# Moving the streamed operands of the second experts to a fixed byte offset from the weights

## The chip, the cores and the metric

The program runs on one core of one Trainium2 chip. The metric is the time of one execution in microseconds on the device. The kernel before takes 1078.79 us, the median of three runs (1077.48 to 1081.04).

## What is computed

Three stages follow each other. An attention of 2 x 8 heads over 576 positions of width 64 adds a far part (on sequences averaged by 4) and a near part (a band of 7 positions). Its result is x, 1152 tokens of width 512. A first feed-forward stage has one inner width of 2048. The second stage, the one that is touched here, has eight experts of inner width 1024, whose outputs are weighted per token by a gate that has been normalised eight times by rows and columns:

```python
# x: 1152 x 512, after attention
h = x @ w_in;  x = (h * tanh(softplus(h))) @ w_out          # first experts
P = normalised(exp(x @ w_gate))                              # 1152 x 8
out = 0
for e in range(8):                                           # second experts
    h = maximum(x @ w1[e], 0.0)
    out += P[:, e:e+1] * (h @ w2[e])
```

## The kernel before

Every fp32 matrix is held as two parts of the type that TensorE multiplies here, a high one and a low one (what the rounding left), and a product of two matrices is three matmuls: high by high, high by low, low by high. TensorE reads two operands from the on-chip memory: the weights, 128 columns that are loaded, and the streamed operand, whose columns (384 or 512 here) run past them. Each matmul has a weight load of its own.

The second experts are worked through in 22 rounds: one of a single piece of 128 inner columns, then 21 of three pieces each. In a round, the three pieces by four blocks of width by three blocks of tokens are multiplied by a scheme with 15 products of sums in place of 18 (`WSUMS`, `XSUMS` and `PROGRAM` name them). A product is six matmuls of 384 columns at line 1505. Its weights are pairs of high and low parts in eight places (`wplace`): four in the tile `wops`, one in `wop0`, two in the tile named `ysum` (`ytile` in the code), and one in `wghl`. Its streamed operand (`operand`) is a block of `xhi` and `xlo`, or a sum of blocks in `xform` or in the tile `xform8` (which the profile's rows also call `xform`, since buffer numbers are left out). ScalarE and VectorE turn the results into `hhi` and `hlo`. After that the second multiplication at line 1553 takes `hhi` and `hlo` as weights, and the streamed operand is a row of the second matrix, split into high and low parts by lines 1368 and 1370, 512 columns each. These rows rotate through three places (`cplace`): the tile `wc` (`wc0` in the code) and two in the tile `xs0`, which is called `late0` in the code and `xs` in the profile's rows. Nine token tiles with nine matmuls each make a round; VectorE adds each result to `yacc` at line 1566.

Before the first round one single piece goes through lines 1338 (its weights lie in `ysum`) and 1348 (the gate, weights in `wghl`).

The order on every engine is written out by a planner (`Plan`), which replays the steps with a table of costs and fixes the order by dependencies. Tiles get their addresses from pools in the order of their allocation. The pool `tp` lies at the upper end and grows downwards, so a tile made larger there moves those allocated ahead of it to lower addresses; in the pool `mp` it moves those allocated after it to higher ones.

In the built program these tiles start at the following bytes of each partition, given modulo 256 (`xhi` and `xlo` are at 0 in both; blocks inside a tile are 512, 1536 or 2048 bytes apart, which changes nothing modulo 256):

```
                                        before   after
weights of the products:   wops              0     192
                           ysum              0     192
                           wop0            192     192
                           wghl            192     192
streamed in the products:  xform           192       0
                           xform8            0       0
weights of line 1553:      hhi, hlo          0       0
streamed at line 1553:     wc                0      64
                           xs (late0)      192      64
```

By "offset" this document means the start of a streamed operand less the start of the weights, modulo 256 bytes. Counted over the program (it is the same count whether a streamed operand is set against its own weights or, but for the last matmul of a product or tile, against those of the next matmul):

```
offset                     0     64    192
line 1505 before         930    210    750
line 1505 after            0   1890      0
line 1553 before         597      0   1140
line 1553 after            0   1737      0
```

Of the kernel before, what the change touches and what calls it, by code (L numbers as in the profile page):

```python
# [9 lines left out]
F32R = mybir.dt.float32r  # L10
# [308 lines left out]
def attn_moe_moe_kernel(  # L319
# [15 lines left out]
    NT, DM = out.shape  # L335
# [3 lines left out]
    KD = DM // 128  # L339
    KH = KD // 2  # L340
# [26 lines left out]
    def new(pool, shape, dt, tag, bufs=2):  # L367
        return pool.tile(shape, dt, tag=tag, name=tag, bufs=bufs)
# [704 lines left out]
    tp = ctx.enter_context(tc.tile_pool(name="tp", bufs=1, side="right", reuse_waits="tile"))  # L1073
    TH = NT // 3
    xform = tp.tile([128, 8, 2, KH, TH], F32R, name="xform")
    xs = [new(tp, [128, KH, NT], F32, f"xs{k}", 1) for k in range(2)]
    wop0 = tp.tile([128, 2, KH, 128], F32R, name="wop0")
    for s in range(ATT_END, NS):
        if s == NS - 4:
            with tc.issue_after(last["mish"].ins):  # L1080
# [17 lines left out]
    mp_, m = [], {}  # L1098
# [13 lines left out]
    for r in range(2):  # L1112
        w1_load(raw1[r].t, rounds_[r])
    ytile = new(yp, [128, KD * NMAX], F32R, "ysum", 1)
    w0 = ytile[:, 0:1024].rearrange("p (z a b) -> p z a b", z=2, a=KD)
    r0 = raw1[0].t[:, 0:512].rearrange("p (a b) -> p a b", a=KD)
    ACT.activation(out=w0[:, 0], in_=r0, func=AF.Copy)
    POOL.tensor_tensor(out=w0[:, 1], in0=r0, in1=f32(w0[:, 0]), op=ALU.subtract)
# [5 lines left out]
    def wplace(i):  # L1124
        if i < 4:
            return m["wops"][:, i]
        if i == 4:
            return wop0
        if i == 7:
            return wghl.rearrange("p (z a) b -> p z a b", z=2)  # L1130
        o = 512 * (i - 5)
        return ytile[:, o:o + 512].rearrange("p (z a b) -> p z a b", z=2, a=KH)

    def cplace(i):
        return m["wc"] if i == 0 else m["late0"][:, 1024 * (i - 1):1024 * i].rearrange("p (z b) -> p z b", z=2)

    def r2place(i):
        return m["temp"][:, 512 * i:512 * i + 512]
# [1 line left out]
    def fplace(z):  # L1140
# [3 lines left out]
        return mt[:, o:o + 768] if z[0] == "m" else m["temp"][:, o:o + 768]  # L1144

    RW, RC, R2 = Ring(8, wplace), Ring(3, cplace), Ring(4, r2place)
    FR = {z: Ring(1, lambda _, z=z: fplace(z).rearrange("p (a b) -> p a b", a=KH)) for z in ("m0", "m1", "r", "t0", "t1", "t2")}
    RK = Ring(6, lambda i: m["keeps"][:, TH * i:TH * i + TH], {"k": 6})
# [146 lines left out]
    def open_():  # L1295
        gq.clear()
        ap_ctx.close()
        mp = ctx.enter_context(tc.tile_pool(name="mp", bufs=1, reuse_waits="tile"))
        mp_.append(mp)
        m["hhi"], m["hlo"] = (mp.tile([128, 3, NT], F32R, name=f"h{z}") for z in ("hi", "lo"))  # L1300
        m["yacc"] = mp.tile([128, NTL, DM], F32, name="yacc")
        m["wc"] = mp.tile([128, 2, DM], F32R, name="wc0")
        m["xform"] = mp.tile([128, 2, KH, TH], F32R, name="xform8")
        m["wops"] = mp.tile([128, 4, 2, KH, 128], F32R, name="wops")
        m["wsums"] = mp.tile([128, len(WSUMS), KH, 128], F32, name="wsums")
        m["temp"] = mp.tile([128, 2304], F32, name="temp")
        m["ones"] = mp.tile([128, 128], F32, name="ones")
        m["P"] = mp.tile([128, 80], F32, name="P")[:, 0:NTL * NE].rearrange("p (a b) -> p a b", b=NE)
    add("open", open_, w=["ap"])

    def late_():
# [43 lines left out]
    def p_rows(r, cs):  # L1355

        out_ = []
        for c in cs:
            z2, y = Buf(R2 if c else FR["t2"]), Buf(RC)
            e, f = divmod(c, NFE)  # L1360
            rk, wk = soon("r2", z2) if c else (["ap"], [])

            def raw(z2=z2, c=c):
                return z2.t if c else z2.t.rearrange("p a b -> p (a b)")[:, 0:DM]
            add("load", lambda raw=raw, e=e, f=f: SP.dma_start(out=raw(), in_=w2[e][128 * f:128 * f + 128, :]), r=rk,
                w=[("r2", c)] + wk, b=[z2], size=262144, rate=0.2)
            rk, wk = soon("c", y)
            add("whi", lambda raw=raw, y=y: ACT.activation(out=y.t[:, 0], in_=raw(), func=AF.Copy), r=[("r2", c)] + rk,  # L1368
                w=[("ch", c)] + wk, b=[z2, y])
            add("wlo", lambda raw=raw, y=y: POOL.tensor_tensor(out=y.t[:, 1], in0=raw(), in1=f32(y.t[:, 0]), op=ALU.subtract),  # L1370
                r=[("r2", c), ("ch", c)], w=[("cl", c)], b=[z2, y])
            out_.append(y)
        return out_

    wc0 = p_rows(0, [0])
# [202 lines left out]
    for r in range(1, len(rounds_)):  # L1578
# [5 lines left out]
        wc = p_rows(r, cs)  # L1584
# [34 lines left out]
```

## Time and profile before

| | before |
|---|---|
| median of three runs | 1078.79 us |
| profiled execution, its own time | 1079.52 us |
| its span, first to last instruction | 1077.7 us |
| TensorE busy | 1051.3 us, 98% of the span |
| VectorE busy | 783.2 us, 73% |
| ScalarE busy | 538.0 us, 50% |
| GpSimd busy | 445.6 us, 41% |
| mean granted clock of TensorE | 0.990 |

The profiled execution took 1.8 us more than its span, and it lies 0.7 us above the median. Matmuls are pipelined, so that a matmul's own duration is longer than the step from its start to the start of the next; how fast TensorE works is read from starts, not from durations.

### The profile page before, as it was taken

To read this page: it belongs to the slowest core of one execution; us is meant where nothing else is said; L and a number is where in the kernel's file an instruction comes from. 1 tells how busy PE (TensorE), PEld (TensorE's weight loads), DVE (VectorE), ACT (ScalarE), POOL (GpSimd) and SP (SyncE) were. 2 spreads that over 40 slices of the span, in tenths; PEclk is the share of its full clock that TensorE was granted. 3 is DMA by queue.
4 is the path that set the end of the run, shared out by engine and by line. 5 is a ranking of instruction groups with operands and counts; after the bars stand their busy time and mean duration, and the time that the engine had idled before them with its cause. 6 is when DMAs were issued, how large, how long until landed. Compare 5 with 4: busy or idle time off the path is not lost.

```text
span 1077.7 us, 18231 instructions
## 1 busy us (share of the span) xinstructions
PE 1051.3 (98%) x6770; PEld 948.5 (88%) x6770; DVE 783.2 (73%) x1394; ACT 538.0 (50%) x1429; POOL 445.6 (41%) x474
## 2 busy tenths in 40 slices
PE   8999999999988899999999999999999999999998
PEld 5799899999887798799889998889889998899887
DVE  6898865442499896887667885798677868687844
ACT  6897874343447354255434643355434544255331
POOL 0343243021158363856335643365335644355311
PEclk9999999999998899999999999999999999999999
DMA  9681222200003210111012111121111111111002
GB/s 208 178 207 47 78 79 81 96 31 30 1 11 97 60 46 33 41 58 55 25 40 60 60 24 48 47 60 36 44 40 59 59 30 50 40 59 30 20 1 88
DMA packets 48000, 63.46 MB, mean 59 GB/s; under 512 B 15272, under 2 KB 31656, under 8 KB 47912
## 3 DMA queue, kind: packets, MB, share of 16 engines
q1 hardware_dynamic: 47912, 62.30, 19.8%
q8 instruction: 53, 0.87, 0.3%
q14 instruction: 35, 0.29, 0.1%
HBM read 59.93 MB, written 2.36 MB: 58 GB/s over the span
## 4 chain that ended last, share of the span: by engine, by line
PE 83%; DVE 11%; ACT 3%; DMA 2%; issue 1%; POOL 0%; SPq 0%; DVEq 0%; ACTq 0%
PE bank L1553 35%; PE bank L1505 25%; PE bank L511 7%; PE bank L530 7%; DVE wsums L1249 3%; PE bank L946 2%; PE bank L1002 2%; DMA raw<-in_moe_w_in_dram 1%; PE bank L660 1%; ACT pl L727 1%; DVE bank L1249 1%; DVE hlo L1326 1%; DMA rawq<-in_q_dram 1%; PE bank L787 1%; PE bank L844 1%
## 5 line engine op out<-in xcount | busy, mean ns | idle before, releaser
L1566 DVE SCALAR_TENSOR_TENSOR yacc<-bank,P,yacc 128x512 f32<-128x512 f32 x208 | 152.8, 745 | 138.9 <-PE bank L1553 138.2
L1553 PE MATMUL bank<-xs,hhi 128*128 128x512 f32 (+1 forms) x760 | 239.6, 396 | 3.4 <-DVE yacc L1564 2.1
L1553 PEld LDWEIGHTS bank<-xs,hhi 128*128 128x128 f32 x760 | 142.4, 189 | 35.0 <-DVE yacc L1564 2.6
L1519 ACT ACTIVATE xs<-bank 128x384 f32<-128x384 f32 x231 | 112.7, 489 | 116.3 <-PE bank L1505 72.4
L1323 ACT ACTIVATE hhi<-bank 128x384 fp32r<-128x384 f32 x150 | 71.8, 488 | 198.0 <-PE bank L1553 193.0
L1553 PE MATMUL bank<-xs,hlo 128*128 128x512 f32 (+1 forms) x380 | 150.3, 396 | 0.0
L1553 PE MATMUL bank<-wc,hhi 128*128 128x512 f32 (+1 forms) x398 | 124.9, 395 | 0.0
L1249 DVE TENSOR_TENSOR bank<-bank,xs 128x384 f32<-128x384 f32 x189 | 101.1, 557 | 20.5 <-ACT xs L1519 16.9
L1505 PE MATMUL bank<-xform,wops 128*128 128x384 f32 x564 | 109.5, 340 | 1.1 <-POOL wops L1480 1.1
L1249 DVE TENSOR_TENSOR wsums<-raws 128x256 f32<-128x256 f32 x147 | 106.1, 743 | 1.4 <-POOL wops L1480 1.4
L1480 POOL TENSOR_TENSOR wops<-wsums,wops 128x256 fp32r<-128x256 f32 x117 | 96.9, 844 | 22.9 <-ACT wops L1478 20.0
L1505 PEld LDWEIGHTS bank<-xform,wops 128*128 128x128 f32 x564 | 100.9, 190 | 3.2 <-POOL wops L1480 1.4
L1370 POOL TENSOR_TENSOR xs<-temp,xs 128x512 fp32r<-128x512 f32 x42 | 54.6, 1304 | 83.9 <-ACT xs L1368 80.4
L1553 PEld LDWEIGHTS bank<-wc,hhi 128*128 128x128 f32 x398 | 74.4, 188 | 16.4
L1480 POOL TENSOR_TENSOR wops<-raws,wops 128x256 fp32r<-128x256 f32 x42 | 35.2, 845 | 125.7 <-ACT wops L1478 125.5
L1553 PEld LDWEIGHTS bank<-xs,hlo 128*128 128x128 f32 x380 | 71.6, 188 | 17.3
L1326 DVE SCALAR_TENSOR_TENSOR hlo<-bank,hhi 128x384 fp32r<-128x384 f32 x150 | 79.6, 549 | 6.3 <-ACT hhi L1323 1.5
L1553 PE MATMUL bank<-wc,hlo 128*128 128x512 f32 (+1 forms) x199 | 78.0, 392 | 0.0
L1505 PE MATMUL bank<-xhi,wops 128*128 128x384 f32 x260 | 74.1, 341 | 0.0
L499 DVE TENSOR_TENSOR glo<-bank,ghi 128x288 fp32r<-128x288 f32 x46 | 20.9, 455 | 71.4 <-ACT ghi L498 71.3
L1505 PE MATMUL bank<-xform,ysum 128*128 128x384 f32 x282 | 56.5, 341 | 0.0
L1480 POOL TENSOR_TENSOR ysum<-wsums,ysum 128x256 fp32r<-128x256 f32 x57 | 47.3, 840 | 18.6 <-ACT ysum L1478 18.1
(239 smaller groups left out, 2493.4 us busy)
## 6 DMA issues: line engine op xcount, KB each, us to landing
temp<-in_moe_w_dram SPq DMA_DIRECT2D x64, 256.0 KB
raws<-in_moe_w_dram SPq DMA_DIRECT2D x16, 768.0 KB
raw<-in_moe_w_in_dram SPq DMA_DIRECT2D x16, 512.0 KB
raw<-in_moe_w_out_dram SPq DMA_DIRECT2D x16, 512.0 KB
raws<-in_moe_w_dram SPq DMA_DIRECT2D x5, 512.0 KB
rawq<-in_q_dram SPq DMA_DIRECT2D x4, 576.0 KB
rawv<-in_v_dram SPq DMA_DIRECT2D x8, 288.0 KB
vw<-in_v_dram SPq DMA_DIRECT2D x12, 192.0 KB
```

The source lines that it names most:

```text
L511: PE.matmul(out=bk, lhsT=a[:, kk, o], rhs=b[:, kk, c0:c0 + n], start=(i == 0), stop=(i == 3 * KD - 1))
L530: PE.matmul(out=bk, lhsT=a[:, h, o], rhs=b, start=(first and i == 0), stop=(end and i == 2))
L946: PE.matmul(out=bk.t[:, 0:n], lhsT=a[:, kk, o], rhs=b[:, kk, c0:c0 + n], start=(i == 0), stop=(i == 3 * KD - 1))
L1249: eng.tensor_tensor(out=out, in0=a, in1=b, op=ALU.add if cb > 0 else ALU.subtract)
L1323: ACT.activation(out=hb.t[0], in_=bk.t[:, 0:TH], func=AF.Relu)
L1326: DVE.scalar_tensor_tensor(out=hb.t[1], in0=bk.t[:, 0:TH], scalar=0.0, in1=f32(hb.t[0]), op0=ALU.max, op1=ALU.subtract)
L1370: add("wlo", lambda raw=raw, y=y: POOL.tensor_tensor(out=y.t[:, 1], in0=raw(), in1=f32(y.t[:, 0]), op=ALU.subtract), r=[("r2", c), ("ch", ...
L1480: add("wl", lambda src=src, y=y: POOL.tensor_tensor(out=y.t[:, 1], in0=piece(src), in1=f32(y.t[:, 0]), op=ALU.subtract), r=key + [("wh", r ...
L1505: PE.matmul(out=bb.t[:, 0:TH], lhsT=y.t[:, wz, kk, :], rhs=x[xz][:, kk, :], start=(fresh and i == 0), stop=(i == 3 * KH - 1), skip_group_c ...
L1519: add("keep", lambda src=src, y=y: ACT.activation(out=y.t, in_=src.t[:, 0:TH], func=AF.Copy), r=[key, "late"], w=[("b", id(y))], b=[src, y])
L1553: PE.matmul(out=bk.t[:, a:b], lhsT=h[hz][:, js], rhs=y[:, wz, a:b], start=(f == fs[0] and i == 0), stop=(f == fs[-1] and i == 2))
L1566: DVE.scalar_tensor_tensor(out=y, in0=bk.t[:, a:b], scalar=p, in1=y, op0=ALU.mult, op1=ALU.add)
```

## The change

Four tiles get spaces in front and the views into them start behind the space; nothing else is edited. `wop0` gets 192 bytes in front, which leaves its own view where it was and moves `xform`, `xs0` and `xs1` down by 192 bytes. The view of `wops` and those into `ysum` start 192 bytes into their tiles. `wc` starts 64 bytes into its tile, and the places in `late0` start 64 bytes into theirs. The tiles behind `wops` in the pool (`wsums`, `temp`, `ones`, `P`) move up by 448 bytes, so that they start at 192 modulo 256. The order of the instructions on all five engines, and what each waits for, is the same, word for word.

```diff
-    wop0 = tp.tile([128, 2, KH, 128], F32R, name="wop0")
+    wop0 = tp.tile([128, 48 + 4 * 128], F32R, name="wop0")[:, 48:].rearrange("p (z a b) -> p z a b", z=2, a=KH)
...
-    w0 = ytile[:, 0:1024].rearrange("p (z a b) -> p z a b", z=2, a=KD)
+    w0 = ytile[:, 48:48 + 1024].rearrange("p (z a b) -> p z a b", z=2, a=KD)
...
-        o = 512 * (i - 5)
+        o = 48 + 512 * (i - 5)
         return ytile[:, o:o + 512].rearrange("p (z a b) -> p z a b", z=2, a=KH)
...
-        return m["wc"] if i == 0 else m["late0"][:, 1024 * (i - 1):1024 * i].rearrange("p (z b) -> p z b", z=2)
+        return m["wc"] if i == 0 else m["late0"][:, 16 + 1024 * (i - 1):16 + 1024 * i].rearrange("p (z b) -> p z b", z=2)
...
-        m["wc"] = mp.tile([128, 2, DM], F32R, name="wc0")
+        m["wc"] = mp.tile([128, 64 + 2 * DM], F32R, name="wc0")[:, 16:16 + 2 * DM].rearrange("p (a b) -> p a b", a=2)
...
-        m["wops"] = mp.tile([128, 4, 2, KH, 128], F32R, name="wops")
+        m["wops"] = mp.tile([128, 48 + 4 * 512], F32R, name="wops")[:, 48:].rearrange("p (i z a b) -> p i z a b", i=4, z=2, a=KH)
```

## Rows read from the trace of the kernel before

**Rows 1.** The page: busy time of each engine, and the granted clock by slices.

```profile
span 1077.7 us, 18231 instructions
PE 1051.3 (98%) x6770; PEld 948.5 (88%) x6770; DVE 783.2 (73%) x1394; ACT 538.0 (50%) x1429; POOL 445.6 (41%) x474
PEclk9999999999998899999999999999999999999999
```

**Rows 2.** The page: the chain that ended last, by engine and by line.

```profile
PE 83%; DVE 11%; ACT 3%; DMA 2%; issue 1%; POOL 0%; SPq 0%; DVEq 0%; ACTq 0%
PE bank L1553 35%; PE bank L1505 25%; PE bank L511 7%; PE bank L530 7%; DVE wsums L1249 3%; PE bank L946 2%; PE bank L1002 2%; DMA raw<-in_moe_w_in_dram 1%; PE bank L660 1%; ACT pl L727 1%; DVE bank L1249 1%; DVE hlo L1326 1%; DMA rawq<-in_q_dram 1%; PE bank L787 1%; PE bank L844 1%
```

**Rows 3.** The chain in order of time (start us, us, what): one round.

```profile
460.44 14.71 PE bank L1505 x84
475.16 16.77 PE bank L1553 x72
...
495.09 14.67 PE bank L1505 x84
```

**Rows 4.** The two longest waits of TensorE from 320 us (total us, times, longest).

```profile
PE bank L1437 <- ACT xs L1519: 4.8, 1, 4.8
PE bank L1505 <- ACT xs L1519: 3.9, 2, 3.7
```

**Rows 5.** Timeline of weight loads, products of one round (start us, us, what).

```profile
495.80 0.19 PEld L1505 LDWEIGHTS bank<-xhi,wops 128*128 128x128 f32 x1
```

**Rows 6.** Timeline of matmuls, products of that round and the matmul before them.

```profile
494.70 0.39 PE L1553 MATMUL bank<-wc,hlo 128*128 128x512 f32 x1
494.93 0.33 PE L1505 MATMUL bank<-xhi,wghl 128*128 128x384 f32 x1
...
495.80 0.34 PE L1505 MATMUL bank<-xhi,wghl 128*128 128x384 f32 x1
495.97 0.35 PE L1505 MATMUL bank<-xhi,wops 128*128 128x384 f32 x1
...
501.20 2.27 PE L1505 MATMUL bank<-xform,ysum 128*128 128x384 f32 x12
503.31 1.21 PE L1505 MATMUL bank<-xform,wghl 128*128 128x384 f32 x6
```

**Rows 7.** Timeline: the first matmul at line 1505 and the last of 512 columns.

```profile
310.80 0.44 PE L1505 MATMUL bank<-xform,wops 128*128 128x384 f32 x1
...
1073.52 0.39 PE L1553 MATMUL bank<-wc,hlo 128*128 128x512 f32 x1
```

**Rows 8.** Matmuls from 550 to 1070 us by form (busy us, mean ns | idle before).

```profile
L1553 PE MATMUL bank<-xs,hhi 128*128 128x512 f32 x560 | 176.0, 395 | 1.3 <-DVE yacc L1566 1.3
L1553 PE MATMUL bank<-wc,hhi 128*128 128x512 f32 x278 | 87.2, 394 | 0.0
L1505 PE MATMUL bank<-xform,wops 128*128 128x384 f32 x384 | 73.3, 337 | 0.0
L1505 PE MATMUL bank<-xhi,wghl 128*128 128x384 f32 x44 | 13.0, 336 | 0.0
```

**Rows 9.** The chain in the first experts: matmuls of 288 columns, line 511.

```profile
177.79 1.58 PE bank L511 x12
...
187.32 1.60 PE bank L511 x12
```

**Rows 10.** The chain from 706 to 721 us, its VectorE stretch (first, last).

```profile
706.43 0.42 DVE hlo L1326
...
720.39 0.67 DVE yacc L1566
```

**Rows 11.** The weights' low halves on GpSimd, 400 to 1070 us, by form.

```profile
L1480 POOL TENSOR_TENSOR wops<-wsums,wops 128x256 fp32r<-128x256 f32 x101 | 82.3, 832 | 12.2 <-ACT wops L1478 11.0 <-PE bank L1505 0.6
L1480 POOL TENSOR_TENSOR wghl<-wsums,wghl 128x256 fp32r<-128x256 f32 x24 | 20.5, 855 | 3.4 <-ACT wghl L1478 3.3
```

**Rows 12.** Waits of ScalarE's split of the second matrix's rows, 320 us on.

```profile
ACT xs L1368 <- PE bank L1553: 21.9, 20, 5.5
```

## The prediction, made before the run

> **What bounds the kernel now.** I read the busy times first: TensorE is busy 98% of the span, VectorE 73%, GpSimd 41%, and the granted clock is near full except for a few slices [rows 1]. The chain that ended last says the same: 83% of it is TensorE, 35% at line 1553 and 25% at line 1505, the two lines that the change touches, and 11% is VectorE [rows 2]. In order of time the chain shows steady rounds: 84 matmuls at line 1505 take 14.67 or 14.71 us (175 ns each), 72 at line 1553 take 16.77 us (233 ns each), with no wait between, and a round takes 34.65 us, from 460.44 to 495.09 [rows 3]. TensorE's longest waits from 320 us on are three, 8.7 us together [rows 4]. So a shorter step from one matmul to the next is what would shorten the time here, and nothing else in the change can.
>
> How long should a step be? From 384 to 512 columns it grows by 58 ns, 0.45 ns a column, close to one tick of the 2.4 GHz clock (0.417 ns), at which 384 columns would take 160 ns and 512 would take 213 ns. The steps are 15 and 20 ns longer. Something costs that much on every matmul, and a clash of two reads is one candidate.
>
> Which reads go on together is seen in the weight loads. The load for the first matmul of the product with `wops` starts at 495.80 us [rows 5], the moment at which the last matmul of the product before it starts [rows 6]. So the weights of the next matmul are fetched while this one streams, and the offset to look at is that between this streamed operand and the next weights. Within a product or a tile that is the offset counted above.
>
> **The change part by part.** No instruction is added, removed or moved, no wait changes. What is left is the step of 1680 products' matmuls (930 at offset 0, 750 at 192) and of 1737 matmuls at line 1553 (597 at 0, 1140 at 192), all of which go to 64.
>
> Line 1505, which has all three offsets already. I took the start of each matmul and of the next one from the timeline (from 310.80 us at line 1505 to 1073.52 at line 1553 [rows 7]), left out steps over 215 ns (275 at line 1553), which hold waits, and averaged by offset. At 64 the step is 173.5 ns (201 steps), at 0 it is 175.5 (878), at 192 it is 175.4 (707). One round shows how small that is against one reading: the product of `xhi` and `wghl`, at 64, goes from 494.93 to 495.97, 173.3 ns a matmul; the two of `xform` and `ysum`, mostly at 192, go from 501.20 to 503.31, 175.8 ns a matmul [rows 6]. The mean durations agree in sign with less: 336 ns for `xhi` with `wghl`, 337 for `xform` with `wops` [rows 8]. I take 2.0 ns, from the steps: 1680 x 2.0 = 3.4 us of TensorE's time. The duration's 1 ns gives the lower end, 1.7 us.
>
> Line 1553, which never has 64 within a tile. There the step is 231.4 ns at 0 (525 steps) and 233.4 at 192 (1109); durations are 394 for `wc` and 395 for `xs` [rows 8]. The nearest rows for 64 are two. At the end of a round the last matmul of 512 columns meets `wghl`, offset 64: 15 steps, 231.3 ns, such as that from 494.70 to 494.93 [rows 6]. And the first experts, with 288 columns, change between 64 and 192 with the token group: twelve matmuls take 1.58 us in a stretch at 64 and 1.60 in one at 192 [rows 9], over all steps of line 511 131.8 ns (284) against 133.2 (218), while line 530 at offset 0 has 132.0. So 64 and 0 are alike there, and 192 costs 1.4 ns more. I take 231.3 ns: 1140 x 2.1 = 2.4 us, and nothing for the 597. The small end is no gain (the 15 steps are few), and a loss is rival D. The large end is a line through the means at 64, 131.8 ns for 288 columns and 173.5 for 384: it gives 229 for 512 columns, so 4.4 ns for 1140 and 2.4 for 597, 6.4 us.
>
> What of this reaches the end: the chain has 0.25 x 1077.7 = 269 us of line 1505, whose 1890 steps take 332 us, so 0.81 of them; and 377 us of line 1553, of 400, so 0.94. The rest lies beside stretches in which VectorE sets the pace, such as 706.43 to 721.06 us [rows 10]; there TensorE would only wait longer. 3.4 x 0.81 + 2.4 x 0.94 = 2.7 + 2.3 = 5.0 us.
>
> Costs elsewhere. GpSimd writes the low halves of weights at 192 instead of 0. Its rows differ by place: 832 ns for `wops` (at 0), 855 for `wghl` (at 192) [rows 11]. For some 200 such operations that is up to 5 us of GpSimd, which is busy for 41% [rows 1] and heads none of TensorE's long waits [rows 4]; I count nothing. VectorE's sums go to `wsums` at 192 instead of 0. No row shows it at another place; GpSimd's 3% is the nearest bound, and on `wsums`' 3% of the chain [rows 2], 32 us, that is 1 us either way; I take nothing. The loads into `temp` land 192 bytes off as before 0; ScalarE, which splits them, waits for TensorE to free its target, not for a load [rows 12], so this is covered.
>
> The profiled execution's 1079.52 us less 5.0 would be 1074.5; it lies 0.7 above the median, so against 1078.79 I predict 1073.8 us, 0.46% less. A difference of 0.3% (3.2 us) is about what a measurement of this kernel can tell from none.
>
> The Trainium skill ("SBUF — State Buffer", section "SBUF: two separate sides") speaks against the whole change: on the engines' side only the port that GpSimd and VectorE share is contended for, and TensorE never waits on anyone. By it where an operand lies would not matter, and the sum would be zero. The trace agrees only in that the effect is small; 131.8 against 133.2 ns between two placements of the same line is a difference that rule doesn't give. That is rival B.
>
> **The rivals.**
>
> A, the forecast: 64 is worth 2 ns a step over 0 and 192 with 384 columns, and with 512 columns it is worth 2 ns over 192 alone. 1073.8 us, between 1071.5 and 1076.
>
> B, nothing changes. The means at line 1505 are of different operands: 64 occurs there only with `wghl` and `wop0` as weights, so the 2 ns may be theirs and not the offset's. Also 15 ns over the columns' time remain at every offset, so the offset plainly isn't the main cause of what is lost. Against it: line 511 shows 64 ahead of 192 with the same tiles, in alternating stretches [rows 9]. 1078.8 us, give or take 1.5.
>
> C, more. With 512 columns the steps fall to 229 ns as on the line above. 2.7 + 6.4 x 0.94 = 8.7 us, so 1070.1 us. For it: at 384 columns 64 does beat 0. Against it: the 15 steps of 512 columns at 64, at 231.3 ns.
>
> D, slower. With `hhi` and `hlo` as weights and 512 columns, 64 is a bad offset: the 525 single steps at offset 0 spread from 224 to 237 ns, so clashes of some 6 ns over the usual do occur. If all 1737 took 236.5 ns, they would lose 3.1 ns on 1140 and 5.1 on 597, 6.6 us, 6.2 of it on the chain, against the 2.7 that line 1505 gives: 1082.3 us. It decides from a step of about 234.3 ns at line 1553, 1.6 above its present mean of 232.7. Against it speak line 511 and the 15 steps.
>
> **How the numbers follow.** A 0.55, B 0.25, C 0.13, D 0.07. The range takes in C's outer end and B: 1068.5 to 1079.5 us; what is left out is most of D and the far edges of B and C. Faster by over 0.3% means below 1075.6 us: C's 0.13, A's 0.46 (its upper edge lies beyond), and 0.02 of B from the runs' scatter, so 0.61. Slower by over 0.3% means above 1082.0: D's upper half and a little of B, 0.05. The rest, 0.34, is within 0.3%.
>
> **What would show it.** In the profile after, the chain's 84 matmuls of line 1505 in a steady round should take about 14.55 us instead of 14.70, 72 of line 1553 about 16.65 instead of 16.77, and a round about 0.3 us less than 34.65. Mean durations should be 336 ns at line 1505 whatever the weights. The first experts should be unchanged. If line 1505 stays at 175 ns a step, the offset is not what made `wghl` and `wop0` faster (B). If line 1553 falls below 16.55 it is C; above 16.87, D. If the steps shrink and the time doesn't, VectorE's stretches have taken the gain: TensorE would wait longer where such a stretch ends, as at 721 us. A granted clock that falls to the lower of its two levels in a steady round, where every slice of the page is at 90% or more [rows 1], would make the prediction wrong from outside the argument.

## The result, and the profile after

The changed kernel takes 1069.18 us (median of four runs, 1067.98 to 1070.7) against 1078.94 before: a ratio of 0.9909 with a 95% interval of 0.9887 to 0.9930, 9.8 us less. The forecast was 1073.8; rival C had 1070.1.

The page after, the lines that answer to [rows 1, 2]:

```profile
span 1066.7 us, 18231 instructions
PE 1040.2 (98%) x6770; PEld 944.2 (89%) x6770; DVE 783.4 (73%) x1394; ACT 538.0 (50%) x1429; POOL 448.4 (42%) x474
PEclk9999999999998999999999999999999999999999
PE 85%; DVE 10%; ACT 2%; DMA 2%; issue 1%; POOL 0%; SPq 0%; DVEq 0%
```

TensorE is busy for 11.1 us less, the span is 11.0 us shorter, and no other engine's busy time moved by more than 3 us. The chain in order of time (start us, us, what), one steady round, beside [rows 3]:

```profile
459.36 14.56 PE bank L1505 x84
473.92 16.49 PE bank L1553 x72
490.41 1.03 PE bank L1505 x6
491.44 2.07 PE bank L1553 x9
493.51 14.56 PE bank L1505 x84
```

84 matmuls of line 1505 went from 14.71 to 14.56 us, where 14.55 was forecast. 72 of line 1553 went from 16.77 to 16.49, 229.0 ns each; the forecast was 16.65, and the sign of rival C, anything below 16.55, was met. A round fell from 34.65 to 34.15 us. The mean durations of the matmuls from 550 to 1060 us, beside [rows 8], are now the same for `xs` and `wc`, and within 1 ns for the products whatever the place of their weights:

```profile
L1553 PE MATMUL bank<-xs,hhi 128*128 128x512 f32 x554 | 172.1, 392 | 0.0
L1553 PE MATMUL bank<-wc,hhi 128*128 128x512 f32 x277 | 86.0, 392 | 0.0
L1505 PE MATMUL bank<-xform,wops 128*128 128x384 f32 x384 | 72.6, 336 | 0.0
L1505 PE MATMUL bank<-xhi,wghl 128*128 128x384 f32 x44 | 13.0, 336 | 0.0
```

From the starts of single matmuls, waits left out as before: line 1505 takes 173.2 ns a step within its products (1787 steps at 64), line 1553 takes 229.2 (1630 steps). Before, the means over all offsets were 175.2 and 232.7. So 1890 x 2.0 + 1737 x 3.5 ns = 3.8 + 6.1 = 9.9 us; with the steps from one line to the other counted in, which hardly gained, it is 9.6. That covers the 9.8 us between the medians. In the two profiled executions the stretch from the first matmul of line 1505 to the last of line 1553 takes 753.2 us instead of 763.5. The first experts, which the change leaves alone, keep their steps: 132.4 ns at line 511 and 132.5 at line 530, before and after. TensorE's waits from 320 us on add up to about 1 us less than before, 13 us against 14:

```profile
PE bank L1505 <- ACT xs L1519: 6.2, 2, 3.7
PE bank L1437 <- DVE P L1421: 4.5, 2, 3.2
PE bank L1553 <- DVE yacc L1564: 2.2, 1, 2.2
PE bank L1505 <- DVE hlo L1326: 0.2, 1, 0.2
```

The waits of the steady rounds, 1.3 us for `yacc` of line 1566 before, are gone. Where the chain had left TensorE for VectorE [rows 10], it now stays (chain, 680 to 725 us, last pieces):

```profile
698.45 13.52 PE bank L1505 x78
711.97 0.69 PE bank L1553 x3
712.66 1.05 PE bank L1505 x6
713.71 11.41 PE bank L1553 x49
```

### The profile page after: what moved, and what is told of

The parts are those of the page before. It is cut to its first block, busy times and chain, and to the rows that moved or that the text cites. A ratio compares the mean times of both kernels' runs of the same rounds, so it can differ in the third digit from the quotient of the medians.

```text
span 1066.7 us, 18231 instructions
## 1 busy us (share of the span) xinstructions
PE 1040.2 (98%) x6770; PEld 944.2 (89%) x6770; DVE 783.4 (73%) x1394; ACT 538.0 (50%) x1429; POOL 448.4 (42%) x474
## 4 chain that ended last, share of the span: by engine, by line
PE 85%; DVE 10%; ACT 2%; DMA 2%; issue 1%; POOL 0%; SPq 0%; DVEq 0%
PE bank L1553 35%; PE bank L1505 28%; PE bank L511 7%; PE bank L530 7%; PE bank L946 2%; PE bank L1002 2%; DVE wsums L1249 2%; DMA raw<-in_moe_w_in_dram 1%; PE bank L660 1%; ACT pl L727 1%; DMA rawq<-in_q_dram 1%; PE bank L787 1%; PE bank L844 1%; DVE bank L1249 1%; DVE hlo L1326 1%
## 5 line engine op out<-in xcount | busy, mean ns | idle before, releaser
L1553 PE MATMUL bank<-xs,hhi 128*128 128x512 f32 (+1 forms) x760 | 236.8, 393 | 2.2 <-DVE yacc L1564 2.2
```

Of the source, the lines that this page charges most:

```text
L1553: PE.matmul(out=bk.t[:, a:b], lhsT=h[hz][:, js], rhs=y[:, wz, a:b], start=(f == fs[0] and i == 0), stop=(f == fs[-1] and i == 2))
```

## The experiments

The theory at first, N: the fetch of the next weights clashes with the streamed operand, and how much depends on the offset alone. Its rivals: the tiles that moved along made the difference (M), or the clash is with what other engines read and write (V).

**The offset alone, with nothing beside it.** The kernel loads one block, and runs 45 matmuls at each of 16 offsets; its core (cut from the file):

```diff
+s = pool.tile([128, 1024 + 64], F32R, name=f"s{z}")[:, 4 * i:4 * i + 1024]     # sa to sp: offset 16 * i bytes
+w = wt[:, 128:256] if i % 3 == 2 else wt[:, 0:128]                             # as in a product: A, A, B
+PE.matmul(out=banks[n // 9 % 8][:, 0:cols], lhsT=w, rhs=s[:, o:o + cols], start=(n % 9 == 0), stop=(n % 9 == 8), skip_group_check=True)
```

> Leaves the whole computation out: 45 matmuls each of 512 and then of 384 columns at 16 offsets (0 to 240 bytes in steps of 16) of the streamed operand from the next weights, with nothing else running beside them. Theory N (the streamed operand and the weights of the next matmul clash where their offset is bad): the step depends on the offset, with about 229 to 230 ns for 512 columns and 173 ns for 384 at 64, and some 2 ns more at 0 and 192 for 384 columns. Rival V (the clash is with what the other engines read and write): without them the step is the same at every offset, and below 229 and 173 ns.

The timeline of its matmuls (start us, us, what); a step is the difference of two starts over the count. Offsets 0, 16, 64, 80, 192 and 208 are `sa`, `sb`, `se`, `sf`, `sm` and `sn`; the first row shown holds the last 14 of the 90 matmuls at 0, from 25 us on, when ScalarE has long filled the tiles (by 19.9 us):

```profile
24.66 3.33 PE L37 MATMUL bank<-sa,wt 128*128 128x512 f32 x14
27.83 10.59 PE L37 MATMUL bank<-sb,wt 128*128 128x512 f32 x45
...
59.25 10.48 PE L37 MATMUL bank<-se,wt 128*128 128x512 f32 x45
69.56 10.55 PE L37 MATMUL bank<-sf,wt 128*128 128x512 f32 x45
...
142.77 10.66 PE L37 MATMUL bank<-sm,wt 128*128 128x512 f32 x45
153.26 10.72 PE L37 MATMUL bank<-sn,wt 128*128 128x512 f32 x45
...
184.82 7.96 PE L37 MATMUL bank<-sa,wt 128*128 128x384 f32 x45
192.62 8.06 PE L37 MATMUL bank<-sb,wt 128*128 128x384 f32 x45
...
216.20 7.96 PE L37 MATMUL bank<-se,wt 128*128 128x384 f32 x45
223.99 7.97 PE L37 MATMUL bank<-sf,wt 128*128 128x384 f32 x45
...
279.04 8.11 PE L37 MATMUL bank<-sm,wt 128*128 128x384 f32 x45
286.99 8.11 PE L37 MATMUL bank<-sn,wt 128*128 128x384 f32 x45
```

512 columns: (69.56 - 59.25) / 45 = 229.1 ns at 64 and 233.1 at 192. V is out: with no other engine at work the step depends on the offset, and at 64 and 192 it has the sizes seen in the kernel. But at 0 it is (27.83 - 24.66) / 14 = 226.4 ns, the least of all sixteen, where N expected no such thing, and 384 columns take 173.3 ns at 0, as at 64. The kernel before had shown 231.4 and 175.5 at 0.

**The changed layout with all offsets at 0, and at 192.** The spaces keep their sizes in sum (what `wop0` gives up lies behind `wghl`), so that every other tile stays put; only `wghl` and the views start elsewhere (shown: at 0, cut; the other kernel has 16 in place of 48 elements for the weights and 48 in place of 16 for the rows):

```diff
-wop0 = tp.tile([128, 48 + 4 * 128], F32R, name="wop0")[:, 48:]...
+wop0 = tp.tile([128, 0 + 4 * 128], F32R, name="wop0")[:, 0:]...
-gl["w"] = wghl = tp.tile([128, KD, 128], F32R, name="wghl")
+gl["w"] = wghl = tp.tile([128, KD * 128 + 48], F32R, name="wghl")[:, 0:KD * 128]...
-m["late0"][:, 16 + 1024 * (i - 1):16 + 1024 * i]
+m["late0"][:, 0 + 1024 * (i - 1):0 + 1024 * i]
...
```

> The changed layout with every offset at 0 instead of 64 in the second experts (other tiles stay where the change put them). Theory N: line 1505 steps 175.5 ns, line 1553 231.4 ns, as before's rows at 0; 1069.2 + 1890 x 2.3 + 1737 x 2.2 ns = 1077.3 us. Rival M (the gain comes from the tiles that moved along, wsums, temp and others): steps as in the changed kernel, 173.2 and 229.2 ns, and 1069 us.

> The changed layout with every offset at 192 in the second experts. Theory N: line 1505 steps 175.4 ns, line 1553 233.4 ns; 1069.2 + 1890 x 2.2 + 1737 x 4.2 ns = 1080.7 us. Rival M: 1069 us.

At 192: 1080.77 us, a ratio of 1.0011 (1.0002 to 1.0021), forecast 1080.7. At 0: 1067.19 us, 0.9894 (0.9875 to 0.9913), and 1069.07 us, 0.9901 (0.9879 to 0.9923), in a second measurement, forecast 1077.3. The chain's steady round at 0:

```profile
472.39 16.36 PE bank L1553 x72
491.89 14.58 PE bank L1505 x84
```

and at 192:

```profile
475.48 16.79 PE bank L1553 x72
495.41 14.84 PE bank L1505 x84
```

M is out: the moved tiles lie alike in both, and 14 us lie between them. Nor does the address of the streamed operand decide by itself. At line 1505 it is 0 (modulo 256) in the changed kernel and in both of these, and only the weights lie elsewhere (192, 0 and 64); in the small kernel the weights stay and the streamed operands move. At offsets of 64 and 192 the steps agree all the same, 173.2 and 176.6 ns here, 173.2 and 176.7 there. But N's "offset alone" fell at offset 0: 174.0 and 227.9 ns a step instead of 175.5 and 231.4.

**The change at line 1505 alone.**

```diff
-m["late0"][:, 16 + 1024 * (i - 1):16 + 1024 * i]
+m["late0"][:, 48 + 1024 * (i - 1):48 + 1024 * i]
-m["wc"] = mp.tile([128, 64 + 2 * DM], F32R, name="wc0")[:, 16:16 + 2 * DM]...
+m["wc"] = mp.tile([128, 64 + 2 * DM], F32R, name="wc0")[:, 0:0 + 2 * DM]...
```

> The change at line 1505 alone: all of its offsets at 64, while line 1553 has wc at 0 and the other two places at 192, as before. Theory N: line 1505 at 173.2 ns, line 1553 back at 231.4 and 233.4; 1890 x 2.0 = 3.8 us of the 9.8 remain, so 1075.1 us. Rival M: 1069 us.

1075.7 us (forecast 1075.1), 0.9966 (0.9938 to 0.9993), and steps of 173.4, 231.2 (at 0) and 233.3 ns (at 192), as N had it. The chain's steady round:

```profile
497.06 14.56 PE bank L1505 x84
511.62 16.76 PE bank L1553 x72
```

So line 1505 alone has 3.8 us of the 9.8, as its steps have, and at line 1553 an offset of 0 between others at 192 is slow again.

**A step depends on the steps before it.** That suggested H: after a switch of offset, matmuls at 0 are slow for a while. In the kernel with all offsets at 0 it can be read from the starts, by the place since the last change of line (means of 43 to 1020 steps, the last before a change left out):

```
offset 0, place since the switch     0      1      2     3-5    6-11   12-23    24 on
line 1505, ns                     170.4  175.9  178.8  179.0  173.4   173.4   173.4
line 1553, ns                     229.3  233.3  235.6  230.1  229.4   226.8   226.8
```

The second small kernel runs `sa` (0), `sb` (64) and `sc` (192) in short alternating runs:

```diff
+runs(10, ("c", 512, 6), ("a", 512, 3))
+runs(6, ("b", 512, 18), ("a", 512, 18))
+runs(6, ("b", 384, 18), ("a", 384, 18))
...
+runs(10, ("a", 384, 6), ("a", 512, 9))
+runs(10, ("b", 384, 6), ("b", 512, 9))
```

> Leaves the whole computation out: matmuls at offsets 0, 64 and 192 alone, in short runs that alternate: 6 at 192 and 3 at 0 (512 columns), 18 at 64 and 18 at 0 (512, then 384 columns), 6 and 6 of 192 and 0 and of 64 and 0 (384 columns), 6 of 384 and 9 of 512 columns at 0, then at 64. Theory H (a step depends on the offsets of the matmuls before it: after a switch to offset 0 some six matmuls are slow, then it settles): the three at 0 after six at 192 take about 231 ns, not the 226.7 of a long run; in the runs of 18 at 0 the first six take about 233 ns (512 columns) and 177 ns (384), the later ones 226.7 and 173.4. Rival O (in the kernel before, what other engines read and write slowed the steps at 0): with nothing beside them short runs are as fast as long ones, 226.7 and 173.4 ns throughout.

Its timeline (start us, us, what; the row at 47.35 is cut off at 50 us):

```profile
32.10 0.85 PE L37 MATMUL bank<-sa,wt 128*128 128x512 f32 x3
32.79 1.56 PE L37 MATMUL bank<-sc,wt 128*128 128x512 f32 x6
34.19 0.86 PE L37 MATMUL bank<-sa,wt 128*128 128x512 f32 x3
34.89 1.56 PE L37 MATMUL bank<-sc,wt 128*128 128x512 f32 x6
...
39.09 4.30 PE L37 MATMUL bank<-sb,wt 128*128 128x512 f32 x18
43.22 4.29 PE L37 MATMUL bank<-sa,wt 128*128 128x512 f32 x18
47.35 2.93 PE L37 MATMUL bank<-sb,wt 128*128 128x512 f32 x12
...
126.25 1.20 PE L37 MATMUL bank<-sc,wt 128*128 128x384 f32 x6
127.29 1.21 PE L37 MATMUL bank<-sa,wt 128*128 128x384 f32 x6
128.34 1.20 PE L37 MATMUL bank<-sc,wt 128*128 128x384 f32 x6
```

Three at 0 after six at 192 take 231.7 ns in the mean of all ten (0.69 and 0.70 us for three in the rows shown), near the 231.4 of the kernel before, with nothing else running: H holds and O falls. Of 18 at 0 the first ten swing between 224 and 236 ns, and from the eleventh on each takes 226 or 227. A change of the column count does the same as a change of offset: six of 384 and nine of 512 columns, all at 0, take 177.2 and 231.2 ns, while all at 64 they take 173.4 and 228.9. An offset of 64 loses less at a switch: the first four of 18 (236.7, 235.0, 231.7 and 231.7 ns) lose some 20 ns against its steady 229, the first ten at 0 some 50 against 226.7. That, and not a better steady step, is its merit over 0. H had the slow stretch as six matmuls. Its length isn't fixed: with 512 columns it was ten in the runs of 18, but three when 45 at 0 followed nine at 64; with 384 columns only the first two of six at 0 between sixes at 192 are slow (176.0 and 181.6 ns). And 192 has no one price either: in those sixes it takes 172.6 ns, less than the 176.7 of its long run. What carries over from one matmul to the next is not shown.

**One edit to the kernel before.** The places in `late0` 64 bytes on, so that all of line 1553 is at 0, line 1505 as it was:

```diff
-m["late0"][:, 1024 * (i - 1):1024 * i]
+m["late0"][:, 16 + 1024 * (i - 1):16 + 1024 * i]
```

> The kernel before with one edit: the two places in late0 start 64 bytes further, so that every offset at line 1553 is 0; line 1505 keeps its mixture. Theory H (at offset 0 the steps of before, 231.4 ns, were slow because only three of nine in a tile were at 0): all of line 1553 falls to about 227.9 ns, 597 x 3.5 + 1140 x 5.5 ns = 8.4 us less than before, a ratio of about 0.992, and line 1505 stays near 175.4. Rival: 231.4 ns is what 512 columns at 0 cost in this layout whatever stands beside them; then only the 1140 gain 2.0 ns, 2.3 us, a ratio of 0.998.

1071.17 us, 0.992 (0.9904 to 0.9937). Line 1553 takes 227.5 ns a step, line 1505 175.3, as before (175.2). The chain's steady round:

```profile
475.49 16.32 PE bank L1553 x72
494.96 14.67 PE bank L1505 x84
```

This one edit has most of the change's gain: 8.6 us, where H had 8.4 and its rival 2.3.

**Line 1505 at 64, line 1553 at 0**, beside the changed kernel and the one with all at 0, on one chip:

```diff
-m["late0"][:, 16 + 1024 * (i - 1):16 + 1024 * i]
+m["late0"][:, 0 + 1024 * (i - 1):0 + 1024 * i]
-m["wc"] = mp.tile([128, 64 + 2 * DM], F32R, name="wc0")[:, 16:16 + 2 * DM]...
+m["wc"] = mp.tile([128, 64 + 2 * DM], F32R, name="wc0")[:, 0:0 + 2 * DM]...
```

> The changed kernel with line 1505 at offset 64 as it is and line 1553 at offset 0. Theory H: line 1505 keeps 173.2 ns a step (at 64 no slow start after a switch), line 1553 takes the 227.9 ns of offset 0; 1737 x 1.3 = 2.3 us less than the changed kernel, about 1067 us, and 1.4 us less than with both at 0. Rival O, or a switch of offsets between the two lines that costs as much as it saves: no less than the faster of the two, 1067 to 1069 us, with line 1553 above 229 ns.

> The changed kernel, unedited, beside the others on the same chip: 173.2 and 229.2 ns a step, a ratio to before of 0.991, as measured.

> Both lines at offset 0, once more beside the others: 174.0 and 227.9 ns a step, 1 us less than the changed kernel, a ratio of 0.990.

1067.13, 1068.48 and 1069.07 us; ratios 0.9882 (0.9859 to 0.9905), 0.9894 (0.9874 to 0.9914) and 0.9901 (0.9879 to 0.9923). The steps are as expected, 173.4 and 227.9 ns in the first (chain):

```profile
472.92 16.36 PE bank L1553 x72
492.40 14.56 PE bank L1505 x84
```

In steps the mixture is the best, 16.36 us for 72 at line 1553 against 16.49 in the changed kernel. In time the three can't be told apart: the intervals overlap, and the kernel with all at 0 alone moved by 1.9 us between two measurements, on two chips. The mixture was expected 2.3 us under the changed kernel and lies 1.4 under it; all at 0 was expected 1 us under it and lies 0.6 above.

## Why the prediction was right, and where it was off

The sign and the place held: no instruction moved, only the step from one matmul to the next fell, at both lines. Of the mechanism, the step does hang on the offset; that each offset has one price, whatever went before, did not hold. The time lies within the range, but only 0.7 us above its lower end, which was drawn to take in rival C. By its own band A, the forecast at 0.55 (1071.5 to 1076), did not come true; C, at 0.13, did, with 1069.2 us against 1070.1 and its sign at line 1553. The forecast gain of 5.0 us was half of the measured 9.8, in three terms.

- Line 1505 was sized right: 3.4 us of TensorE's time forecast, 3.8 measured. The reason given was partly wrong. 64 is not 2 ns better than 0 as such; in the kernel before, steps at 0 come in runs that a switch keeps interrupting. Six steps or more into a run at 0 they took 173.3 ns there too (203 steps).
- The term of line 1553 was mis-sized: 2.4 us forecast, 6.1 measured. The step that failed is "I take 231.3 ns", from 15 steps of 512 columns at 64. Each was a single step at 64, behind a tile of six at 192 and three at 0, and it carried their price: in the kernel with the one edit, where line 1553 is at 0 throughout, the 15 at the same place take 228.6 ns. In the changed kernel, too, the first step of line 1553 after the products takes 232.4 ns (57 steps), those from the fourth on 229. The line through 288 and 384 columns, which I kept as the large end, gave 229. "Nothing for the 597" fell with it: their 231.4 ns was the price of three steps between six at 192, not of offset 0.
- The factor for what reaches the end, 0.81 and 0.94 from the chain's shares, should have been 1: the steps' 9.6 to 9.9 us are the 9.8 measured. In the steady rounds before, TensorE had waited for VectorE for only 1.3 us in all [rows 8], so the stretches in which the chain ran along VectorE cost TensorE next to nothing, and after the change they did not hold it back. Why VectorE was no longer late there was not tried.
- The costs elsewhere were rightly taken as nothing. GpSimd's busy time rose by 2.8 us, beside other work; its rows for `wops` and `wghl`, now both at 192, take 842 and 843 ns.
- Rival B fell with the kernels at 0 and 192. The Trainium skill's rule behind it ("SBUF — State Buffer", section "SBUF: two separate sides") is that TensorE never waits on anyone. By it the place of an operand would make no difference; here the same matmul of 512 columns took 226.7 to 234.6 ns with no other engine at work. That it is TensorE's two reads that clash was the thought behind the change; the runs show what the place does, not that. Rival D fell with 229.2 ns (of its 525 single steps at offset 0 three took 241 ns, over the 237 given).
- That the weights that count are those of the next matmul is not settled. It rests on the weight load that starts with the matmul before it [rows 5, 6]. Where a product's last matmul is followed by line 1553, the offset to the next weights is 0 in the changed kernel, with all at 192 and with all at 0; the steps are 176.5, 173.6 and 175.6 ns (57 to 58 of each). So the next weights alone do not set the step, and with all at 0, where no offset changes, the change of the column count moves it too.

## What to carry to other kernels

Where TensorE's stream of matmuls has no gaps, read the step from start to start and group it by the place of the streamed operand against the next weights, modulo 256 bytes (that it repeats after 256 was taken, not tried); 1 to 2% of the step hung on it in this kernel, up to 4% in the small one. Choose the value and make it the same for all matmuls in a row: either alone may gain nothing. All at 192 took 1080.77 us, no less than the mixture before, and 0 among 192 took 231.4 ns where 0 throughout took 227.9. When such a group is read from a mixed stream, split it by the place since the last switch, or the mixture is taken for the value.

## What the runs showed of the hardware that was not expected

- The step of a matmul depends on the matmuls before it. After a change of offset, steps at offset 0 range from 224 to 236 ns (512 columns) for ten matmuls in the runs of 18 and for three in the last run, and then settle at 226 to 227.
- Of 16 offsets in steps of 16 bytes, in long runs of one execution of the small kernel, 0 and 64 are the best for 512 columns (226.7 and 229.2 ns), the other fourteen lie between 231.0 and 234.6. For 384 columns seven lie between 173.2 and 173.5 (0, 32, 64, 80, 112, 160, 224) and 240 is the worst with 179.7.
- No offset comes nearer than 13 ns to the 213 ns that 512 columns would take at one column a tick of 2.4 GHz. What the remaining 13 ns are was not tried.
